# Two 64-row matmuls on different rows of the array for the low weights' half chunk of a score sum

## The chip, the core and the metric

The kernel runs on one core of one Trainium2 chip. The core has five engines with queues of their own: TensorE (PE, with its weight loads shown as PEld), VectorE (DVE), ScalarE (ACT), GpSimd (POOL, which here issues the gathers) and SyncE (SP, which issues the plain loads and stores). All DMA queues share 16 DMA engines. The metric is the device time of one execution in microseconds (us).

## What is computed

The input is x, 2048 tokens of 576 numbers. The output mixes two branches with a gate per token:

```python
g = sigmoid((x * gate_w).sum(-1, keepdims=True))
a = irfft2(rfft2(x) * (w_r + 1j * w_i))             # over tokens and features
q = einsum("nd,dhc->nhc", x, w_q)                   # 32 heads, 2 x 128 each
s1 = einsum("nhd,ed->nhe", q[..., :128], k1)        # 64 scores
s2 = einsum("nhd,ed->nhe", q[..., 128:], k2)        # 64 scores
e  = argmax(s1) * 64 + argmax(s2)                   # one expert per token and head
act = gelu(einsum("nd,nhd->nh", x, u[e]))
b = einsum("nh,nhd->nd", act, v[e])
out = g * a + (1 - g) * b
```

(The softmax runs over a single candidate, so its weight is 1.) An argmax that falls on another expert would change the output, so the scores need nearly full fp32 accuracy. u and v are stored side by side, so one gathered row of 1152 numbers serves both.

## The kernel before

**Tiles and chunks.** The tokens make 16 tiles t of 128. The 32 heads make 8 chunks c of 4 heads, so a chunk has 4 x 2 x 64 = 512 scores for a token. The 576 features make four chunks i = 0 to 3 of 128 and a half chunk i = 4 of 64.

**Weights.** `build_m(c, i)` multiplies the query weights by the keys into M, feature rows by 512 score columns, so that scores = x M. It works in fp32 on column halves of the array (the output on partitions 0 to 63 or 64 to 127, line p<-kT,uv in the profile). M is kept in two fp32r parts, `mh` (the rounded value) and `ml` (the rest); tiles named mhx and mlx are the same thing in other buffers. For i = 4 the 64 feature rows are laid down twice (`load_wq` copies them), so partitions 0 to 63 and 64 to 127 of `mh` hold the same, and of `ml` too.

**Tokens.** `load_x(b, i)` loads the transposed x for a block b of 512 tokens and splits it in the same way: ACT writes the rounded part (line 417), DVE the rest (line 418). For i < 4 these are two tiles. For i = 4 they share one tile, xts[8]: rounded part on partitions 0 to 63, rest on 64 to 127.

**Scores.** `scores(c, tp)` does two tiles, the members j = 0 and 1 of pair tp, into one PSUM buffer of two banks, a bank for each member. There are 8 x 8 = 64 such pairs. For i < 4 a member has three matmuls of 128 tokens by 512 columns (x hi with mh, x hi with ml, x lo with mh). For i = 4 it has two: the stacked tile with `mh` gives hi and lo at once, and the stacked tile with `ml` gives hi with ml (and the negligible lo with ml). That makes 14 matmuls for a member and 28 for a pair, 1792 in all. The token tile is the stationary operand, so each matmul loads 128 columns of weights first. Behind the matmuls stand a maximum on DVE (line 503), sign marks on ACT (line 511) and the search for the index of the maximum.

**Experts.** `group(t, c)` gathers four rows (line 637, tiles 0 to 9), `quad(t, c)` does it for tiles 10 to 15 (line 744; none is issued before the last score pair has begun). DVE takes the dot product with x (lines 649 and 753). The sum over v goes through DVE (line 681), or through a scaling on ACT and an addition on DVE (lines 674 and 675, the groups in `A_OF`), or through TensorE with a diagonal matrix: full width (128*128) for most groups in `D_OF`, on 64 columns for the tiles in `PAIR` (0 and 1), on 32 columns for the quads.

**The Fourier branch** (`fold`, `unit_front`, `unit_back`, `invert`) runs behind the scores, beside the quads.

**The order.** All steps are jobs made by `plan(...)`, with an assumed duration. A long list, `ORDER`, then says in which order they are issued; each engine takes its own jobs strictly in that order. The assumed durations were used to find the list and change no instruction. The 64 score pairs, the weight products and the diagonal matmuls thus stand in one fixed row on TensorE.

Of the kernel before, what the change touches and what calls it, by code (L numbers as in the profile page):

```python
# [19 lines left out]
P = 128  # L20
# [82 lines left out]
FIRST = 1.0  # L103
# [155 lines left out]
def act(n):  # L259
    return 0.1 + n / 1250  # L260
# [10 lines left out]
def load(nbytes, row):  # L271
    return nbytes / row * (0.01 + row * 0.0000363) / 16
# [3 lines left out]
def tile_kernel(ctx, tc, xn, xT, x5, wqT, wq5, kT, wri, uv, gw, t_kr, t_ff, t_fv, t_tw, t_io, out):  # L276
# [131 lines left out]
    def load_x(b, i, at, at2, n=1):  # L408
        st = buf("uv", ROW, view=lambda x: x.rearrange("p a d -> p (a d)")[:, : n * 512])
        h = P if i < 4 else E  # L410
        src = lambda: xT[:, i, b * 512 : (b + n) * 512] if i < 4 else x5[:, b * 512 : (b + n) * 512]
        ld(load(h * n * 2048, n * 2048) * FIRST, at, lambda: nc.sync.dma_start(st.ap[:h], src()), [st])
        for m in range(n):
            hi = xts[i if i < 4 else 8][b + m]
            lo, r = (xts[4 + i][b + m], 0) if i < 4 else (hi, E)
            cut = lambda m=m: st.ap[:h, m * 512 : m * 512 + 512]
            ac(act(512), at2, lambda hi=hi, cut=cut: actv(hi.ap[:h], cut(), AF.Copy), [hi], [st])  # L417
            dv(dve(512), at2, lambda hi=hi, lo=lo, cut=cut: vt(lo.ap[r : r + h], cut(), hi.ap[:h].bitcast(F32), ALU.subtract), [lo], [st, hi])
# [54 lines left out]
    def scores(c, tp, at):  # L473
# [6 lines left out]

        def part(j, i):
            t = 2 * tp + j
            b = t // 4
            tsl = slice((t % 4) * P, (t % 4) * P + P)
            mh, ml = m_t[c, i]
            x = xts[i if i < 4 else 8][b]
            seq = [(x, mh), (x, ml)] + ([(xts[4 + i][b], mh)] if i < 4 else [])

            def go():
                for n, (xx, m) in enumerate(seq):  # L490
                    mm(ps.ap[:, j, :], xx.ap[:, tsl], m.ap, start=i == n == 0, stop=i == 4 and n == len(seq) - 1)

            use = {id(q): q for pair in seq for q in pair}
            return plan("PE", 0.2275 * len(seq), at, go, [(ps, j)], list(use.values()))

        seq = [(j, i) for i in range(ND) for j in range(2)] if tp in (0, 7) else [(j, i) for j in range(2) for i in range(ND)]
        js = [part(j, i) for j, i in seq]
# [45 lines left out]
        for a, b, kind in runs(ta, tb):  # L543
# [3 lines left out]
            elif kind == "pair":  # L547
                for j, q, to, at_ in halves_of(ei[c], a, b):
                    ac(0.15, at + O_EI, lambda a=a, b=b, j=j, q=q, to=to: actv(
                        to(), fe.ap[64 * j : 64 * j + 64, a - ta : b - ta, q::2], AF.Copy, scale=float(E)), [(ei[c], t, j, q) for t in range(a, b)], [fe])  # L550
# [38 lines left out]
    def soften(c, t0, t1, at):  # L589
# [5 lines left out]
        def move():  # L595
            for a, b, kind in runs(t0, t1):
# [3 lines left out]
                else:  # L600
                    for j, q, to, _ in halves_of(moved, a, b):
                        ac(0.15, at, lambda a=a, b=b, j=j, q=q, to=to: actv(
# [27 lines left out]
    def group(t, c, at, ahead, gate_by=(), ks=range(HPC), mixed=False):  # L630
# [58 lines left out]
        for h in range(2 if t in PAIR else 0):  # L689
            dg = buf("dg", [P, 2, P // 2])  # L690
            for j in range(2):
                ac(0.2, at + O_DG, lambda j=j, h=h, dg=dg: actv(dg.ap[:, j, :], ip, AF.Copy, scale=a.ap[:, 2 * j + h : 2 * j + h + 1]), [(dg, j)], [a, "ip"])
# [459 lines left out]
A_OF = {2: (0, 1, 4), 3: (6,), 4: (3,), 5: (0, 2, 4, 7), 6: (0, 1, 2, 3, 4), 9: (0,)}  # L1152
# [276 lines left out]
```

## Time and profile before

| | |
|---|---|
| median of 3 runs | 937.85 us (936.73 to 946.15) |
| the profiled execution | 938.13 us |
| its span, first to last instruction | 936.4 us |
| busy, share of the span: PE / DVE / ACT / POOL | 91% / 88% / 70% / 60% |
| moved by DMA | 345.77 MB, of it 302.02 MB by gathers |
| HBM traffic over the span | 368 GB/s |

Busy time of PE is to be read with care: matmuls are pipelined, the record of a 128x512 matmul is about 0.39 us long while the next one starts after 0.23 us. So the prediction goes by distances between starts. In a timeline row stand the start, the length and the number of merged instructions; a form such as 128*64 128x288 means 128 rows and 64 columns of the array, and 288 columns streamed. An fp32 matmul leaves two records, an fp32r matmul one. PEld rows are the weight loads.

### The profile page before, as it was taken

The page shows a single profiled execution, that of the slowest core. Times are in us where ns is not written, and L with a number is a line of the kernel's source. Part 1 is how long each engine was busy: PE and PEld are TensorE (multiplying, and loading weights), DVE is VectorE, ACT ScalarE, POOL GpSimd, SP SyncE. Part 2 cuts the span into 40 slices and gives each one's busy share as a digit, 9 for nine tenths or more (in the row PEclk, how much of TensorE's full clock was granted, in tenths as well). Part 3 has the DMA queues.
Part 4 walks back from the last instruction along what each step waited for, and adds up shares of the span by engine and source line. Part 5 has one row for each costly group of instructions (what it writes and reads, how often), then busy time and mean ns, then how long its engine had stood idle before and what let it go on. Part 6 is the DMA issues. An engine that isn't in the chain of part 4 may idle for free.

```text
span 936.4 us, 17794 instructions
## 1 busy us (share of the span) xinstructions
PE 853.8 (91%) x5878; PEld 634.9 (68%) x5878; DVE 821.0 (88%) x1997; ACT 653.4 (70%) x2292; POOL 559.9 (60%) x516
## 2 busy tenths in 40 slices
PE   6999999999999999999999984687788779899997
PEld 5687887887877887887877872454455446566775
DVE  3585899999899999999989998998788889998887
ACT  3799999788887797977787899736338272634633
POOL 0234465665567666656656764777676667557762
PEclk9999999999999999999999997889899989999999
DMA  8967989989999999999999999999999999999998
GB/s 277 366 226 232 373 315 339 376 324 378 361 308 412 403 354 396 365 379 330 380 331 406 345 385 398 365 406 398 409 369 417 420 416 417 417 403 387 413 419 356
DMA packets 91261, 345.77 MB, mean 369 GB/s; under 512 B 10208, under 2 KB 10848, under 8 KB 91168
## 3 DMA queue, kind: packets, MB, share of 16 engines
q0 software_dynamic: 73728, 302.02, 83.7%
q1 hardware_dynamic: 17440, 42.60, 12.8%
q8 instruction: 47, 0.77, 0.3%
q14 instruction: 46, 0.38, 0.1%
HBM read 339.86 MB, written 4.72 MB: 368 GB/s over the span
## 4 chain that ended last, share of the span: by engine, by line
PE 60%; DMA 14%; DVE 12%; ACT 7%; issue 4%; POOL 2%; SPq 0%; DVEq 0%; ACTq 0%; POOLq 0%
PE p L346 60%; DMA uv<-uv,eiq 9%; DVE uv L753 4%; DMA uv<-xT 2%; ACT xr L734 2%; POOL uv L744 2%; ACT sg L511 2%; DMA uv<-uv,ei 1%; DVE uv L649 1%; DVE xn L681 1%; DMA xn<-xn 1%; DVE t L968 1%; DVE t L969 1%; POOL uv L637 1%; DMA uv<-wqT 1%
## 5 line engine op out<-in xcount | busy, mean ns | idle before, releaser
L637 POOL DMA_INDIRECT uv<-uv,ei x320 | 353.0, 1103 | 267.7 <-PE p L346 55.9
L346 PE MATMUL p<-mh,xt 128*128 128x512 f32 x768 | 263.4, 398 | 0.0
L744 POOL DMA_INDIRECT uv<-uv,eiq x192 | 206.7, 1077 | 93.4 <-PE p L346 39.3
L511 ACT ACTIVATE sg<-p,mx 128x64 bf16<-128x64 f32 x1024 | 230.9, 349 | 27.7 <-DVE mx L503 25.1
L649 DVE SCALAR_TENSOR_TENSOR uv<-uv,xn 128x576 f32<-128x576 f32 x320 | 232.8, 751 | 17.4 <-DMA uv<-uv,ei 13.9
L346 PE MATMUL p<-uv,dg 128*32 128x288 f32 (+2 forms) x1264 | 167.5, 430 | 41.6 <-DVE dg L759 23.3
L346 PE MATMUL p<-ml,xt 128*128 128x512 f32 x448 | 175.1, 391 | 1.0 <-DVE ml L467 1.0
L346 PEld LDWEIGHTS p<-mh,xt 128*128 128x128 f32 x768 | 144.2, 188 | 33.7 <-issue 3.1
L753 DVE SCALAR_TENSOR_TENSOR uv<-uv,xr 128x576 f32<-128x576 f32 x192 | 139.7, 754 | 18.8 <-DMA uv<-uv,eiq 18.2
L346 PEld LDWEIGHTS p<-uv,dg 128*32 128x32 f32 (+2 forms) x1264 | 85.6, 135 | 103.2 <-DVE dg L759 33.0
L346 PE MATMUL p<-mhx,xt 128*128 128x512 f32 x384 | 135.6, 400 | 0.9 <-ACT xt L417 0.9
L681 DVE SCALAR_TENSOR_TENSOR xn<-uv,a,xn 128x576 f32<-128x576 f32 x132 | 107.2, 812 | 2.3 <-ACT xn L677 1.3
L346 PEld LDWEIGHTS p<-ml,xt 128*128 128x128 f32 x448 | 84.2, 188 | 17.5 <-DVE ml L467 1.4
L503 DVE TENSOR_REDUCE mx<-p 128x16 f32<-128x1024 f32 x64 | 78.0, 1219 | 10.8 <-PE p L346 10.6
L346 PEld LDWEIGHTS p<-mhx,xt 128*128 128x128 f32 x384 | 72.0, 188 | 21.7 <-issue 3.5
L522 ACT ACTIVATE sg<-sg 128x256 bf16<-128x256 bf16 x192 | 75.3, 425 | 1.1
L346 PE MATMUL p<-mlx,xt 128*128 128x512 f32 x192 | 75.1, 391 | 0.0
L756 ACT ACTIVATE b<-z 128x4 f32<-128x4 f32 x48 | 9.9, 205 | 82.8 <-DVE uv L753 82.6
L734 ACT ACTIVATE xr<-xl 32x576 f32<-32x576 f32 x96 | 65.4, 681 | 1.4
L346 PEld LDWEIGHTS p<-kT,uv 128*64 128x64 f32 x1280 | 42.2, 143 | 19.5 <-issue 7.8
L346 PE MATMUL p<-kT,uv 128*64 128x64 f32 x1280 | 47.2, 230 | 6.9 <-ACT kT L787 6.3
L346 PE MATMUL p<-kr,f 128*32 128x128 f32 (+1 forms) x384 | 44.3, 328 | 9.5 <-DVE f L899 8.3
(127 smaller groups left out, 1139.8 us busy)
## 6 DMA issues: line engine op xcount, KB each, us to landing
uv<-wqT SPq DMA_DIRECT2D x32, 512.0 KB, 7.2
uv<-uv,ei POOLq DMA_INDIRECT x320, 6.8
w<-wri SPq DMA_DIRECT2D x16, 289.0 KB, 6.2
out<-xn SPq DMA_DIRECT2D x16, 288.0 KB, 5.6
uv<-uv,eiq POOLq DMA_INDIRECT x192, 7.8
xn<-xn SPq DMA_DIRECT2D x8, 288.0 KB, 5.3
tw<-t_tw SPq DMA_DIRECT2D x9, 256.0 KB, 6.7
uv<-xT SPq DMA_DIRECT2D x8, 256.0 KB, 6.9
```

The lines of the kernel that those rows point to most:

```text
L346: after("PE", nc.tensor.matmul(*args, **kw))
L503: dv(dve(1024, True), at + O_MAX + nd("m", c, tp), lambda: nc.vector.tensor_reduce(mv.ap[:, 2 * tp : 2 * tp + 2, :], ps.ap.rearrange("p a ...
L511: on("ACT", actv(sg.ap[:, j, g, :], ps.ap[:, j, g * E : g * E + E], AF.Sign, bias=mv.ap[:, 2 * tp + j, g : g + 1], scale=-1.0))
L522: ac(act(256), at + O_ADD, lambda b=b: actv(s2()[:, :, b * Q : b * Q + Q], s2()[:, :, b * Q : b * Q + Q], AF.Copy, bias=b / 4), [sg], [])
L637: on("POOL", nc.gpsimd.indirect_dma_start(out=g.ap.rearrange("p a d -> p (a d)"), out_offset=None, in_=uv, in_offset=bass.IndirectOffsetOn ...
L649: dv(0.68, at + O_DOT + nd("d", t, c), lambda k=k, g=rows[k], xk=xk: stt(g.ap[:, 0, :], g.ap[:, 0, :], 1.0, xk.ap, op0=ALU.mult, op1=ALU.m ...
L681: dv(0.73, at + O_SUM + nd("v", t, c), lambda v=v, s=s: stt(y.ap, v(), s(), y.ap, op0=ALU.mult, op1=ALU.add), [y], [(rows[k], 1), a])
L734: ac(0.69, at + 0.6 * j, lambda j=j, q=q: actv(xr[t][j].ap[QB * q : QB * q + QB, :], x.ap[QB * j : QB * j + QB, :], AF.Copy), [(xr[t][j], ...
L744: on("POOL", nc.gpsimd.indirect_dma_start(out=g.ap.rearrange("p a d -> p (a d)"), out_offset=None, in_=uv, in_offset=bass.IndirectOffsetOn ...
L753: dv(0.68, at + O_QDOT + nd("d", t, c), lambda j=j: stt(rows[j].ap[:, 0, :], rows[j].ap[:, 0, :], 1.0, xr[t][j].ap, op0=ALU.mult, op1=ALU. ...
L756: ac(0.12, at + O_QGELU, lambda: actv(b.ap, z.ap, AF.Gelu_apprx_tanh), [b], [(z, j) for j in range(HPC)], table="gelu")
L968: dv(dve(578, True), at, lambda: vt(a.ap, p.ap[:, :, :DF], w.ap[:, 0:1, :].to_broadcast([P, 2, DF]), ALU.mult), [(a, 0), (a, 1)], [p, w])
```

## The change

Three things change in the program. The half chunk's tile xts[8] is laid out by member: for the even tile of a pair the rounded part is on partitions 0 to 63 and the rest on 64 to 127, for the odd tile it is the other way round. The input x5 is stored accordingly (128 partitions of 256 columns a block, where it was 64 of 512), and two ACT and two DVE instructions of half the width make the split where one of each did. In `scores` the two steps for i = 4 become one, `both()`, at the end of the pair: a full matmul with `mh` for each member, then for each member a matmul with `ml` over 64 rows alone, rows 0 to 63 for j = 0 and rows 64 to 127 for j = 1, into their two banks. Third, `ORDER` is another list, and two groups, (2, 4) and (6, 1), leave `A_OF`. Some assumed durations (FIRST, 0.15 to 0.2, 0.2 to 0.24) change, which changes no instruction by itself.

```diff
     def load_x(b, i, at, at2, n=1):
-        h = P if i < 4 else E
-        src = lambda: xT[:, i, b * 512 : (b + n) * 512] if i < 4 else x5[:, b * 512 : (b + n) * 512]
...
+        w = 512 if i < 4 else 256
+        src = lambda: (xT[:, i] if i < 4 else x5)[:, b * w : (b + n) * w]
...
+            if i == 4:
+                x = xts[8][b + m]
+                of = lambda j, r, x=x: x.ap[E * r : E * r + E].rearrange("p (a j q) -> p a j q", j=2, q=P)[:, :, j, :]
+                own = lambda j, cut=cut: cut()[E * j : E * j + E].rearrange("p (a q) -> p a q", q=P)
+                for j in range(2):
+                    ac(act(256), at2, lambda j=j, of=of, own=own: actv(of(j, j), own(j), AF.Copy), [x], [st])
+                for j in range(2):
+                    dv(dve(256), at2, lambda j=j, of=of, own=own: vt(of(j, 1 - j), own(j), of(j, j).bitcast(F32), ALU.subtract), [x], [st])
+                continue
...
     def scores(c, tp, at):
...
-            seq = [(x, mh), (x, ml)] + ([(xts[4 + i][b], mh)] if i < 4 else [])
+            seq = [(xb(i), mh), (xb(i), ml), (xb(4 + i), mh)]
...
+        def both():
+            mh, ml = m_t[c, 4]
+            x = xb(8)
+            def go():
+                for j in range(2):
+                    mm(ps.ap[:, j, :], x.ap[:, tsl[j]], mh.ap, start=False, stop=False)
+                for j in range(2):
+                    mm(ps.ap[:, j, :], x.ap[E * j : E * j + E, tsl[j]], ml.ap[E * j : E * j + E], start=False, stop=True)
+            return plan("PE", 0.2275 * 3, at, go, [(ps, 0), (ps, 1)], [x, mh, ml])
...
-        seq = [(j, i) for i in range(ND) for j in range(2)] if tp in (0, 7) else [(j, i) for j in range(2) for i in range(ND)]
-        js = [part(j, i) for j, i in seq]
+        seq = [(j, i) for i in range(4) for j in range(2)] if tp in (0, 7) else [(j, i) for j in range(2) for i in range(4)]
+        js = [part(j, i) for j, i in seq] + [both()]
...
-A_OF = {2: (0, 1, 4), 3: (6,), 4: (3,), 5: (0, 2, 4, 7), 6: (0, 1, 2, 3, 4), 9: (0,)}
+A_OF = {2: (0, 1), 3: (6,), 4: (3,), 5: (0, 2, 4, 7), 6: (0, 2, 3, 4), 9: (0,)}
```

More of the change, by code (lines that the diff above doesn't have):

```diff
@@ L102 @@
 WINDOW, LOW, HIGH = 3.4133, 0.52, 0.86
-FIRST = 1.0
+FIRST = 1.1
 LAND = {'POOL': 0.2, 'SP': 5.29}
@@ L408, in load_x @@
     def load_x(b, i, at, at2, n=1):
-        st = buf("uv", ROW, view=lambda x: x.rearrange("p a d -> p (a d)")[:, : n * 512])
-        h = P if i < 4 else E
-        src = lambda: xT[:, i, b * 512 : (b + n) * 512] if i < 4 else x5[:, b * 512 : (b + n) * 512]
-        ld(load(h * n * 2048, n * 2048) * FIRST, at, lambda: nc.sync.dma_start(st.ap[:h], src()), [st])
-        for m in range(n):
[L414 to L418, printed above, removed]
+        w = 512 if i < 4 else 256
+        h = P
+        st = buf("uv", ROW, view=lambda x: x.rearrange("p a d -> p (a d)")[:, : n * w])
+        src = lambda: (xT[:, i] if i < 4 else x5)[:, b * w : (b + n) * w]
+        ld(load(P * n * w * 4, n * w * 4) * FIRST, at, lambda: nc.sync.dma_start(st.ap, src()), [st])
+        for m in range(n):
+            cut = lambda m=m: st.ap[:, m * w : m * w + w]
+            if i == 4:
[7 more added lines that the diff above has]
+                continue
+            hi, lo, r = xts[i][b + m], xts[4 + i][b + m], 0
+            ac(act(512), at2, lambda hi=hi, cut=cut: actv(hi.ap, cut(), AF.Copy), [hi], [st])
+            dv(dve(512), at2, lambda hi=hi, lo=lo, cut=cut: vt(lo.ap, cut(), hi.ap.bitcast(F32), ALU.subtract), [lo], [st, hi])
     def load_xn(t, tag, at, after=()):
@@ L479, in scores @@
         ps = psum()
+        tsl = [slice((2 * tp + j) % 4 * P, (2 * tp + j) % 4 * P + P) for j in range(2)]
+        xb = lambda i: xts[i][tp // 2]
         def part(j, i):
@@ L483, in part @@
             b = t // 4
-            tsl = slice((t % 4) * P, (t % 4) * P + P)
             mh, ml = m_t[c, i]
-            x = xts[i if i < 4 else 8][b]
-            seq = [(x, mh), (x, ml)] + ([(xts[4 + i][b], mh)] if i < 4 else [])
+            seq = [(xb(i), mh), (xb(i), ml), (xb(4 + i), mh)]
             def go():
                 for n, (xx, m) in enumerate(seq):
-                    mm(ps.ap[:, j, :], xx.ap[:, tsl], m.ap, start=i == n == 0, stop=i == 4 and n == len(seq) - 1)
+                    mm(ps.ap[:, j, :], xx.ap[:, tsl[j]], m.ap, start=i == n == 0, stop=False)
             use = {id(q): q for pair in seq for q in pair}
             return plan("PE", 0.2275 * len(seq), at, go, [(ps, j)], list(use.values()))
-        seq = [(j, i) for i in range(ND) for j in range(2)] if tp in (0, 7) else [(j, i) for j in range(2) for i in range(ND)]
-        js = [part(j, i) for j, i in seq]
+        def both():
[9 more added lines that the diff above has]
+        js = [part(j, i) for j, i in seq] + [both()]
         score_jobs[c, tp] = js
@@ L548, in scores @@
                 for j, q, to, at_ in halves_of(ei[c], a, b):
-                    ac(0.15, at + O_EI, lambda a=a, b=b, j=j, q=q, to=to: actv(
+                    ac(0.2, at + O_EI, lambda a=a, b=b, j=j, q=q, to=to: actv(
                         to(), fe.ap[64 * j : 64 * j + 64, a - ta : b - ta, q::2], AF.Copy, scale=float(E)), [(ei[c], t, j, q) for t in range(a, b)], [fe])
@@ L601, in move @@
                     for j, q, to, _ in halves_of(moved, a, b):
-                        ac(0.15, at, lambda a=a, b=b, j=j, q=q, to=to: actv(
+                        ac(0.2, at, lambda a=a, b=b, j=j, q=q, to=to: actv(
                             to(), cand.ap[64 * j : 64 * j + 64, a - t0 : b - t0, q::2], AF.Copy, bias=1.0), [(moved, a, j, q)], [cand])
@@ L691, in group @@
             for j in range(2):
-                ac(0.2, at + O_DG, lambda j=j, h=h, dg=dg: actv(dg.ap[:, j, :], ip, AF.Copy, scale=a.ap[:, 2 * j + h : 2 * j + h + 1]), [(dg, j)], [a, "ip"])
+                ac(0.24, at + O_DG, lambda j=j, h=h, dg=dg: actv(dg.ap[:, j, :], ip, AF.Copy, scale=a.ap[:, 2 * j + h : 2 * j + h + 1]), [(dg, j)], [a, "ip"])
             def go(h=h, dg=dg):
@@ L1403, in _layout @@
     arrays = {
-        "xn": xn, "xT": c(xt[: 4 * P].reshape(4, P, S).transpose(1, 0, 2)), "x5": c(xt[4 * P :]),
+        "xn": xn, "xT": c(xt[: 4 * P].reshape(4, P, S).transpose(1, 0, 2)), "x5": c(xt[4 * P :].reshape(E, 8, 2, P).transpose(2, 0, 1, 3).reshape(P, 8 * P)),
         "wqT": c(w[..., : 4 * P].reshape(NCH, P, 8, 4, P).transpose(0, 3, 1, 2, 4)), "wq5": c(w[..., 4 * P :].reshape(NCH, P, 512)), "kT": c(np.concatenate([k1, k2, k1], 1)), "wri": c(wri),
```

352 rows, old and new, of the table ORDER are left out of this document.

## The prediction, made before the result was known

> **What bounds the kernel now.** I read the windows first (two stretches, cut at the last score matmul), then the timeline of PE around that cut, then the starts of single matmuls.
>
> ```profile
> core 0: us, PE busy (x) PEld busy (x) DVE busy (x) ACT busy (x) POOL busy (x), PEclk, DMA share, GB/s
> 45.00:558.00 513.00, 512.24 (x3242) 402.08 (x3243) 474.99 (x1076) 432.98 (x1719) 308.50 (x280) 1.00 0.94 351
> 558.00:936.00 378.00, 306.58 (x2337) 204.84 (x2335) 327.59 (x890) 194.36 (x504) 246.41 (x228) 0.95 1.01 401
> ```
>
> ```profile
> 44.86 200.78 PE p L346 x1379
> ...
> 269.27 265.86 PE p L346 x1636
> ```
>
> ```profile
> 557.68 0.39 PE L346 MATMUL p<-ml,xt 128*128 128x512 f32 x1
> ```
>
> ```profile
> 599.15 0.94 POOL L744 DMA_INDIRECT uv<-uv,eiq  x1 [1.40 <-PE p L346]
> ```
>
> From 45 to 558 us TensorE is without a hole (512.24 of 513 us, granted clock 1.00), and the chain of waits goes through it in two long pieces of 200.78 and 265.86 us. At 557.68 the last score matmul starts. The quads of the six late tiles follow, the first at 599.15. In that second stretch PE has holes (306.58 of 378), DMA has none (share 1.01) and moves 401 GB/s, against 351 before. So TensorE sets when the scores are done, and DMA the length of what comes behind. A microsecond that a score pair gains or loses on PE moves the cut, and the rest of the kernel follows as far as its work is locked to the scores.
>
> **The price of a matmul inside a dense row.** The four groups of score matmuls count 768 + 448 + 384 + 192 = 1792, that is 28 for each of 64 pairs.
>
> ```profile
> L346 PE MATMUL p<-mh,xt 128*128 128x512 f32 x768 | 263.4, 398 | 0.0
> L346 PE MATMUL p<-ml,xt 128*128 128x512 f32 x448 | 175.1, 391 | 1.0 <-DVE ml L467 1.0
> L346 PE MATMUL p<-mhx,xt 128*128 128x512 f32 x384 | 135.6, 400 | 0.9 <-ACT xt L417 0.9
> L346 PE MATMUL p<-mlx,xt 128*128 128x512 f32 x192 | 75.1, 391 | 0.0
> ```
>
> ```profile
> 307.43 0.39 PE L346 MATMUL p<-mhx,xt 128*128 128x512 f32 x1
> ...
> 308.79 0.39 PE L346 MATMUL p<-mhx,xt 128*128 128x512 f32 x1
> ```
>
> From 307.43 to 308.79 are six steps: 1.36 / 6 = 0.227 us each. The records are 0.39 us long, but 0.227 is what a matmul costs.
>
> **The change, step 1: one streaming time saved.** A pair now sends its two `ml` matmuls one behind the other, 0.454 us. If two 64-row halves run side by side they take 0.227. The saving is 0.227 a pair, 64 x 0.227 = 14.5 us.
>
> **Step 2: going to half rows and back.** No matmul of this trace uses fewer than 128 rows, so the price of the switch has to be bounded. The nearest rows are those that use half the columns: the diagonal matmuls of tiles 0 and 1. They stand between score matmuls, in blocks of 8 and of 16 records.
>
> ```profile
> 293.74 0.39 PE L346 MATMUL p<-mhx,xt 128*128 128x512 f32 x1
> 294.06 1.19 PE L346 MATMUL p<-uv,dg 128*64 128x288 f32 x8
> 295.18 0.50 PE L346 MATMUL p<-mhx,xt 128*128 128x512 f32 x1
> 295.52 0.40 PE L346 MATMUL p<-mlx,xt 128*128 128x512 f32 x1
> ```
>
> ```profile
> 355.60 0.39 PE L346 MATMUL p<-mh,xt 128*128 128x512 f32 x1
> 355.92 2.16 PE L346 MATMUL p<-uv,dg 128*64 128x288 f32 x16
> ...
> 358.35 0.40 PE L346 MATMUL p<-ml,xt 128*128 128x512 f32 x1
> ```
>
> ```profile
> 294.06 0.68 PEld L346 LDWEIGHTS p<-uv,dg 128*64 128x64 f32 x8 [0.35 <-issue]
> 295.18 0.19 PEld L346 LDWEIGHTS p<-mhx,xt 128*128 128x128 f32 x1 [0.44 <-issue]
> 295.29 0.19 PEld L346 LDWEIGHTS p<-mlx,xt 128*128 128x128 f32 x1
> ```
>
> From the score matmul ahead of the block to the second one behind it are 295.52 - 293.74 = 1.78 us; without the two score matmuls (0.454) the block of 8 costs 1.326. The block of 16 costs 358.35 - 355.60 - 0.454 = 2.296. The difference, 0.97, is the streaming of 8 records, so each block pays 1.326 - 0.97 = 0.356 us beside its streaming. The same matmuls at full width show that the switch is what costs:
>
> ```profile
> 302.24 0.40 PE L346 MATMUL p<-mhx,xt 128*128 128x512 f32 x1
> 302.48 1.13 PE L346 MATMUL p<-uv,dg 128*128 128x288 f32 x4
> 303.23 0.61 PE L346 MATMUL p<-mh,xt 128*128 128x512 f32 x1
> 303.68 0.39 PE L346 MATMUL p<-ml,xt 128*128 128x512 f32 x1
> ```
>
> ```profile
> 331.72 0.39 PE L346 MATMUL p<-ml,xt 128*128 128x512 f32 x1
> 331.95 2.10 PE L346 MATMUL p<-uv,dg 128*128 128x288 f32 x8
> ...
> 334.12 0.39 PE L346 MATMUL p<-mlx,xt 128*128 128x512 f32 x1
> ```
>
> Here 4 records cost 303.68 - 302.24 - 0.454 = 0.986 and 8 cost 334.12 - 331.72 - 0.454 = 1.946: 0.24 a record and 0.026 left over. Two things follow. Column halves do run side by side (8 records in 0.97 us instead of 1.92). And nothing is paid at full width, since weights are loaded under the matmul ahead. At a switch they aren't: the first weight load starts at 294.06, 0.32 us behind the start at 293.74, so 0.09 us after that stream has ended; on the way back the load starts at 295.18 and the next load at 295.29, so 128 columns of weights take an open 0.11 us.
>
> For half rows the lower end is no price at all (loads go on in the background, only the rows differ), the upper end the same switch with more load in the open: the stationary operand has 128 columns where the blocks had 64, so half of 0.11 comes on top: 0.356 + 0.055 = 0.41 us. If the second half's load waits for the first, another 0.11. I take 0.41, since the column halves are the only partial use of the array here. A pair's tail then takes 0.41 + 0.227 = 0.637 where it took 0.454: +0.183 us, 64 x 0.183 = +11.7 us. The saving is eaten above a switch price of 0.227.
>
> [...]
>
> **Step 3: switches that fall together.** Where a two-row step stands directly beside a column block, one way back and one way in become one, half of 0.356, some 0.18 us less.
>
> ```profile
> L346 PE MATMUL p<-kT,uv 128*64 128x64 f32 x1280 | 47.2, 230 | 6.9 <-ACT kT L787 6.3 <-DMA uv<-wqT 0.7
> L346 PE MATMUL p<-uv,dg 128*64 128x288 f32 x256 | 40.3, 434 | 9.7 <-ACT dg L692 9.7
> ```
>
> There are 1280 / 32 = 40 weight products and 256 / 8 = 32 diagonal blocks, 72. With 9 steps to a pair, 128 of 576 places border a two-row step; at random 16 would meet, fewer since some blocks stand together. I take 11: -2 us.
>
> **Step 4: the layout of the half chunk.** The bytes loaded and the number of issues on SP stay. ACT and DVE get one more instruction for each of four token blocks.
>
> ```profile
> L418 DVE TENSOR_TENSOR xt<-uv,xt 128x512 fp32r<-128x512 f32 (+1 forms) x20 | 13.2, 687 | 18.0 <-ACT xt L417 18.0
> ```
>
> One of 512 columns takes 0.687; two of 256 take between 0.687 and twice that, so 0 to 0.7 us a block. Only the first block can be on the path (PE's dense row begins at 45 us; the others are loaded under it): 0 to 0.7, I take +0.2.
>
> **Step 5: two groups leave A_OF.** Eight ACT scalings go, eight DVE additions become multiply-adds.
>
> ```profile
> L674 ACT ACTIVATE uv<-uv,a 128x576 f32<-128x576 f32 x56 | 40.9, 784 | 3.1 <-DVE a L662 2.9
> L675 DVE TENSOR_TENSOR xn<-uv,xn 128x576 f32<-128x576 f32 x56 | 42.1, 752 | 0.9 <-ACT uv L674 0.3
> L681 DVE SCALAR_TENSOR_TENSOR xn<-uv,a,xn 128x576 f32<-128x576 f32 x132 | 107.2, 812 | 2.3 <-ACT xn L677 1.3
> ```
>
> ACT loses 8 x 0.784 = 6.3 us, DVE gains 8 x (0.812 - 0.752) = 0.5 us of its 475 in 513. PE covers both: 0. Without that cover, +0.5.
>
> **Step 6: the new order.** It moves every queue's jobs, POOL's and SP's too, but makes no new work. In the first stretch PE has no hole that an order could close. In the second DMA is full. I give it 0, between -4 and +4: that is 1% of the 378 us behind the cut, whose DMA rows are at their limit; a worse order would show as holes there.
>
> **The sum.** The cut moves by 11.7 - 2 + 0.2 = +9.9. What is behind it keeps its length, because each engine's order is fixed: dots, diagonal matmuls and gathers take their turns between the score pairs. From the profiled execution (span 936.4, 1.7 around it, 938.1; 0.3 above the median 937.85): 938.1 + 9.9 = 948.0 us.
>
> **The rivals.**
>
> No drain for rows (faster). Half rows are loaded in the background and the whole 14.5 us come: the mechanism is that only the rows differ and no column's path does. For it: column halves run side by side at full gain once they run. Against: loads at a switch of columns wait. It decides below a price of 0.227. The cut moves by -14.5; DVE then has 475 in 498 (95%) and DMA must give 351 x 513 / 498 = 362 GB/s, under the 401 seen. Between all of it and two thirds: 924 to 929. [...]
>
> One side only. The way in is hidden, the way back costs its 0.09 + 0.11 = 0.20: 0.227 - 0.20 leaves 0.03 a pair, -2 us: 936. For it: nothing seen; against: both ways wait in the column rows.
>
> Dearer. The two loads go one behind the other: +0.11 x 64 = 7 us, 955. Or the halves don't run side by side, so that the saving fails: +14.5, 962.5.
>
> Absorbed. PE loses 10 us, but gathers go on meanwhile and fewer are left behind the cut.
>
> ```profile
> POOL uv L637 <- PE p L346: 55.6, 43, 5.1
> ```
>
> ```profile
> q0 software_dynamic: 73728, 302.02, 83.7%
> ...
> L637 POOL DMA_INDIRECT uv<-uv,ei x320 | 353.0, 1103 | 267.7 <-PE p L346 55.9
> ...
> L744 POOL DMA_INDIRECT uv<-uv,eiq x192 | 206.7, 1077 | 93.4 <-PE p L346 39.3
> ```
>
> In the first stretch 280 of the 320 gathers of line 637 are issued, so up to 40 come later; a gather is 302.02 / (320 + 192) = 0.59 MB, or 1.5 us of DMA at 401 GB/s. Seven more of them done would give back all 10 us: 938 to 941. Against: POOL waited 55.6 us there for buffers that PE frees, in PE's fixed order.
>
> **How the numbers follow.** Forecast 0.42 (own range 943 to 953); dearer 0.18 (953 to 963); absorbed 0.09; one side 0.11; no drain 0.20 (924 to 930). About 1% (9.4 us) is what a measurement can tell from no change; the border at 947.2 runs through the forecast, two thirds of it above. Slower by over 1%: 0.28 + 0.18 = 0.46. Within 1%: 0.14 + 0.09 + 0.11 = 0.34. Faster: 0.20. The range, 929 to 962, takes in the top of the fast case and nearly all of the dear one.
>
> **What would show it.** Step 1: the two 64-row matmuls start within some 10 ns. Step 2: the 64-row weight load starts 0.3 us behind the last full matmul, and from that matmul to the second one behind the pair it is 0.637 + 0.454 = 1.09 us; 0.68 would mean no drain. Step 3: fewer than 64 such ways back. The sum: the last score matmul at about 568 us, with no hole on PE before it, and some 378 us behind it. The prediction is wrong if PE's row gets holes, if the half rows load in the background, or if the part behind the cut changes its length by more than 4 us.

## The result and the profile after

The changed kernel took 946.78 us in the median of 12 runs (946.09 to 953.36). The kernel before, timed beside it, took 939.75 (12 runs, 936.73 to 946.15). The ratio is 1.0085 with a 95% interval of 1.0068 to 1.0103, so the change costs 7 us. The forecast was 948.0.

The profiled execution of the changed kernel took 949.5 us, 2.7 above its own median. The one of before (938.13) is 1.6 under its median. The two profiles are therefore further apart (11.4 us) than the kernels.

The windows of the changed kernel, cut at its last score matmul as those of before were (columns: length, then busy us and instructions of each engine, granted clock, DMA share, GB/s):

```profile
45.00:568.70 523.70, 520.62 (x3247) 388.70 (x3245) 477.50 (x1074) 427.83 (x1711) 303.53 (x282) 1.00 0.93 346
568.70:947.30 378.60, 309.47 (x2338) 208.23 (x2336) 325.20 (x892) 194.23 (x504) 246.78 (x228) 0.92 1.01 400
```

Its timeline of PE, first at the last score step, then around the two-row step of one pair, with the weight loads of the same place:

```profile
568.50 0.50 PE L346 MATMUL p<-ml,xt 64*128 64x512 f32 x2
```

```profile
103.02 0.84 PE L346 MATMUL p<-mh,xt 128*128 128x512 f32 x3
103.80 0.50 PE L346 MATMUL p<-ml,xt 64*128 64x512 f32 x2
104.23 0.50 PE L346 MATMUL p<-mh,xt 128*128 128x512 f32 x1
104.56 0.39 PE L346 MATMUL p<-ml,xt 128*128 128x512 f32 x1
```

```profile
103.79 0.18 PEld L346 LDWEIGHTS p<-ml,xt 64*128 64x128 f32 x2 [0.35 <-issue]
104.22 0.19 PEld L346 LDWEIGHTS p<-mh,xt 128*128 128x128 f32 x1 [0.25 <-issue]
104.33 0.19 PEld L346 LDWEIGHTS p<-ml,xt 128*128 128x128 f32 x1
```

The last score matmul starts at 568.50, 10.8 us later than before. PE is nearly as dense as it was up to there: its holes are 523.7 - 520.62 = 3.1 us, against 0.8 in the kernel before. What follows is as long as it was (378.6; before 378.5 from its cut at 557.9). So most of the loss lies in PE's own work, ahead of the cut.

The step itself reads so. The third matmul of the merged row ends at 103.02 + 0.84 = 103.86, so it starts 0.39 earlier, at 103.47. The 64-row load comes at 103.79, 0.32 us later, with nothing but [<-issue] as the reason for the idle time. The two half matmuls share one row of 0.50 us, as long as one of them alone, so they start together; in the records of all 64 pairs the second starts 3 or 4 ns behind the first. The load on the way back is at 104.22, the second full matmul at 104.56: 1.09 us from 103.47, where four matmuls in a dense row take 4 x 0.227 = 0.91.

### The profile page after: what moved, and what is told of

It reads as the page before. It is cut to its first block, busy times and chain, and to the rows that moved or that the text cites. A ratio compares the mean times of both kernels' runs of the same rounds, so it can differ in the third digit from the quotient of the medians.

```text
span 947.3 us, 17772 instructions
## 1 busy us (share of the span) xinstructions
PE 864.8 (91%) x5878; PEld 623.9 (66%) x5878; DVE 820.5 (87%) x2001; ACT 649.2 (69%) x2288; POOL 554.2 (59%) x516
## 4 chain that ended last, share of the span: by engine, by line
PE 54%; DMA 16%; DVE 12%; ACT 10%; issue 4%; POOL 2%; SPq 0%; DVEq 0%; ACTq 0%; POOLq 0%
PE p L346 54%; DMA uv<-uv,eiq 7%; DMA uv<-uv,ei 6%; DVE uv L775 3%; ACT xr L756 3%; DMA uv<-xT 2%; ACT sg L533 2%; DVE uv L671 2%; POOL uv L659 1%; POOL uv L766 1%; DVE xn L703 1%; ACT fl L952 1%; DMA uv<-wqT 1%; DVE xn L1122 1%; ACT uv L696 1%
## 5 line engine op out<-in xcount | busy, mean ns | idle before, releaser
L659 POOL DMA_INDIRECT uv<-uv,ei x320 | 346.6, 1083 | 285.3 <-PE p L346 74.8
L346 PE MATMUL p<-mh,xt 128*128 128x512 f32 x768 | 257.2, 401 | 1.2 <-ACT mh L467 0.6
L671 DVE SCALAR_TENSOR_TENSOR uv<-uv,xn 128x576 f32<-128x576 f32 x320 | 234.0, 752 | 21.5 <-DMA uv<-uv,ei 16.8
L346 PE MATMUL p<-ml,xt 128*128 128x512 f32 (+1 forms) x448 | 157.2, 422 | 0.1
L346 PE MATMUL p<-mhx,xt 128*128 128x512 f32 x384 | 138.2, 407 | 0.5 <-ACT xt L426 0.3
L703 DVE SCALAR_TENSOR_TENSOR xn<-uv,a,xn 128x576 f32<-128x576 f32 x140 | 113.8, 814 | 1.5 <-ACT xn L699 0.2
L346 PEld LDWEIGHTS p<-ml,xt 128*128 128x128 f32 (+1 forms) x448 | 72.1, 187 | 33.7 <-issue 21.6
L346 PE MATMUL p<-kr,f 128*32 128x128 f32 (+1 forms) x384 | 47.0, 337 | 2.3 <-DVE f L921 1.6
```

The lines of the kernel that those rows point to most:

```text
L346: after("PE", nc.tensor.matmul(*args, **kw))
L659: on("POOL", nc.gpsimd.indirect_dma_start(out=g.ap.rearrange("p a d -> p (a d)"), out_offset=None, in_=uv, in_offset=bass.IndirectOffsetOn ...
L671: dv(0.68, at + O_DOT + nd("d", t, c), lambda k=k, g=rows[k], xk=xk: stt(g.ap[:, 0, :], g.ap[:, 0, :], 1.0, xk.ap, op0=ALU.mult, op1=ALU.m ...
L703: dv(0.73, at + O_SUM + nd("v", t, c), lambda v=v, s=s: stt(y.ap, v(), s(), y.ap, op0=ALU.mult, op1=ALU.add), [y], [(rows[k], 1), a])
```

## The experiments

Four runs went to one chip, on which the kernel before took 939.69 us. All later runs went to another, on which it took 976 to 992 us; those are read against the kernel before of the same chip. "Cut" is the start of the last score matmul in the profile.

**Undo the half rows.** In the last step of the changed kernel:

```diff
-                    mm(ps.ap[:, j, :], x.ap[E * j : E * j + E, tsl[j]], ml.ap[E * j : E * j + E], start=False, stop=True)
+                    mm(ps.ap[:, j, :], x.ap[:, tsl[j]], ml.ap, start=False, stop=True)
```

> The changed kernel, order and layout included, with the two products of ml over all 128 rows again (the stacked tile with ml, as before), so 28 full matmuls a pair and no half rows. Theory A (the loss is the price of switching between full and half rows, 0.41 us a pair against 0.227 saved): each pair's tail takes 0.18 us less, 64 x 0.18 = 11.5, less about 1 us since five of the switches met a column block; 946.8 - 10.5 = 936 us, the last score matmul at about 558 us. Rival B (the half rows cost nothing; the loss came with the new order and layout): 946 to 948 us.

Measured: 939.21 us, ratio to the kernel before 0.9994 (0.9974 to 1.0014); cut at 561.3. The new order and layout with full matmuls are as fast as the old, so Rival B is out: the half rows carry the whole loss of 946.78 - 939.21 = 7.6 us. But 7.6 is less than the 10.5 expected. The cut came only 7.2 us earlier than in the changed kernel. Here PE waits, in us in total, times, longest, from 45 us to the cut:

```profile
PE p L346 <- ACT sg L533: 1.7, 3, 1.2
PE p L346 <- ACT mh L467: 0.9, 2, 0.8
PE p L346 <- ACT dg L725: 0.7, 1, 0.7
PE p L346 <- ACT mlx L474: 0.6, 1, 0.6
```

These rows of the waits view sum to 3.9 us. The changed kernel has 2.7 up to its own cut, and the kernel before 0.8:

```profile
PE p L346 <- ACT sg L533: 1.9, 3, 1.2
PE p L346 <- ACT mlx L474: 0.5, 1, 0.5
PE p L346 <- ACT dg L725: 0.3, 1, 0.3
```

So the waits are some 1.2 us of what is missing; the rest is not explained. The profiled execution of e1_full took 944.42 us, 5.2 above its median, so its cut is a late one.

**The saving without the price.**

```diff
-                for j in range(2):
-                    mm(ps.ap[:, j, :], x.ap[E * j : E * j + E, tsl[j]], ml.ap[E * j : E * j + E], start=False, stop=True)
+                mm(ps.ap[:, 0, :], x.ap[:, tsl[0]], ml.ap, start=False, stop=True)
```

> Like e1_full, but the product of the half chunk's rounded x with ml is left out for the odd member of each pair: 27 full matmuls, no half rows. It is what the change would cost if two half rows took one streaming time and the switch nothing. Theory A (what TensorE loses or gains in the score stage passes to the end): 64 x 0.227 = 14.5 us under e1_full, so 921.5 us if A is right on e1_full. Rival C (DVE or DMA take over as the bound once PE is faster): 926 us or more, with holes in PE's row before the last score matmul.

Measured: 933.63 us, ratio 0.9924 (0.9898 to 0.9951), 5.6 us under e1_full; cut at 552.9. Of 14.5 us taken from PE, 5.6 reach the end. In the two profiles the cut comes 8.4 us earlier and the executions are 8.6 apart (935.85 and 944.42), so the profiles are further apart than the medians; behind the cut both are as long (380.6 and 380.8). The longest waits of PE up to the cut:

```profile
PE p L346 <- ACT mh L467: 3.4, 2, 2.1
PE p L346 <- ACT sg L532: 2.6, 4, 1.2
PE p L346 <- ACT dg L724: 1.2, 1, 1.2
PE p L346 <- ACT dg L713: 1.1, 2, 0.5
```

ACT ends these (8.3 us here, 3.9 in e1_full), and in the window up to the cut ACT is busy 426.51 of 508.1 us and DMA's share is 0.95:

```profile
45.00:553.10 508.10, 499.25 (x3182) 394.05 (x3180) 475.07 (x1073) 426.51 (x1708) 307.52 (x280) 1.00 0.95 356
```

So Rival C was right about the size and the holes. The instructions that end PE's waits are ACT's, which it had not named, but that does not rule out DVE or DMA behind them. ACT itself waits in this window mostly for DVE, and so it did just ahead of PE's longest wait:

```profile
ACT b L674 <- DVE uv L670: 27.9, 21, 5.4
ACT sg L532 <- DVE mx L524: 21.2, 20, 3.3
```

```profile
456.39 0.93 ACT L532 ACTIVATE sg<-p,mx 128x64 bf16<-128x64 f32 x4 [2.59 <-DVE mx L524]
```

```profile
458.98 0.50 PE L346 MATMUL p<-mh,ident 128*128 128x256 f32 x2 [2.08 <-ACT mh L467]
```

Whether ACT's own fixed order or DVE ahead of it makes the holes was not tried.

**The same switch, one half only.** As e2_one_full, with `x.ap[:E, ...]` and `ml.ap[:E]` for the one matmul that is left.

> Like the changed kernel, but the ml product of the odd member is left out: one 64-row matmul a pair, on rows 0 to 63, so it has the same switches and no second half. It differs from e2_one_full only in the rows of that one matmul. Theory A (the halves run wholly side by side; the price is the switch): the same time as the changed kernel, 946 to 948 us, and 64 x 0.41 = 26 us, less about 1, above e2_one_full. Rival D (part of the price is the second half, its load or its streaming): shorter than the changed kernel by up to 14.5 us, 932 us at the least.

Measured: 947.05 us, ratio 1.0084 (1.0054 to 1.0115). That is the time of the changed kernel, so the second half costs nothing. It is 13.4 us over e2_one_full, where 25 to 26 were expected. On PE the price is what was expected:

```profile
102.23 0.61 PE L346 MATMUL p<-mh,xt 128*128 128x512 f32 x2
102.78 0.50 PE L346 MATMUL p<-ml,xt 64*128 64x512 f32 x1
103.21 0.50 PE L346 MATMUL p<-mh,xt 128*128 128x512 f32 x1
103.54 0.39 PE L346 MATMUL p<-ml,xt 128*128 128x512 f32 x1
```

The last full matmul starts at 102.23 + 0.61 - 0.39 = 102.45, the second one behind the half at 103.54: 1.09 us with one half as with two. Without a switch these three steps take 0.68, so the price is 0.41. In time it shows as about half. In part that is because e2_one_full could not use its saving: up to the cut PE has 8.9 us of holes there and 3.2 here. The rest of the difference was not followed.

**The change in the old order.** The kernel before with only the new layout and the half rows, sent behind the last step of the pair:

```diff
+                if i == 4:
+                    mm(ps.ap[:, j, :], x.ap[:, tsl], mh.ap, start=False, stop=False)
+                    seen.append(j)
+                    for k in range(2 if len(seen) == 2 else 0):
+                        u = (2 * tp + k) % 4 * P
+                        mm(ps.ap[:, k, :], x.ap[E * k : E * k + E, u : u + P], ml.ap[E * k : E * k + E], start=False, stop=True)
+                    return
```

> The kernel before, with its order, A_OF and assumed durations, and only the half chunk's layout and the two 64-row matmuls of the change: they are sent right behind whichever of the two members' last steps comes second. Theory A with the new order counted in: the score pairs pay 64 x 0.18 = 11.5 us, less 0.2 for each place where the two-row step meets a column block; the old order has 55 separate column blocks before the last score matmul where the new one has 42 (at 0.35 us each the new order saves 4.6 us): 939.75 + 11.5 - 1 = 950 us. Rival E (the orders are worth the same): 946 to 948 us. Rival B (half rows free): 940 us.

Measured: 948.97 us, ratio 1.0090 (1.0062 to 1.0118); cut at 568.1, 10.4 us later than in the kernel before. In the old order 9.3 us of the loss reach the end (the cuts are of single profiles, the times medians). That the new order is worth the 2.2 us between 948.97 and 946.78 is not shown: the two intervals overlap widely.

**Two switches a pair.**

```diff
                 for j in range(2):
                     mm(ps.ap[:, j, :], x.ap[:, tsl[j]], mh.ap, start=False, stop=False)
-                for j in range(2):
                     mm(ps.ap[:, j, :], x.ap[E * j : E * j + E, tsl[j]], ml.ap[E * j : E * j + E], start=False, stop=True)
```

> The changed kernel with the four matmuls of the last step in another sequence: full for the even member, its 64 rows, full for the odd member, its 64 rows. Two ways in and two ways back a pair, and no half runs beside the other. Theory A (every way in and back is paid, whatever stands around it): a pair takes another 0.41 + 0.227 = 0.637 us less about 0.003, 64 x 0.634 = 40.6 us on PE; the last score matmul at 568.5 + 40.6 = 609 us and the time 947 + 40 = 987 us. Rival F (a switch is paid once for a pair, by the first matmul of another form): only the lost overlap, 64 x 0.227 = 14.5 us, 961 us. Rival G (the stretch behind the scores gets shorter as gathers go on meanwhile): last score matmul at 609 us, but 975 us or less.

Measured: 1029.88 us where the kernel before took 986.15, ratio 1.0426 (1.0373 to 1.0480).

```profile
113.05 0.50 PE L346 MATMUL p<-ml,xt 64*128 64x512 f32 x1
113.47 0.49 PE L346 MATMUL p<-mh,xt 128*128 128x512 f32 x1
113.90 0.49 PE L346 MATMUL p<-ml,xt 64*128 64x512 f32 x1
114.32 0.50 PE L346 MATMUL p<-mh,xt 128*128 128x512 f32 x1
```

Every change between half and full rows costs again: 0.42 to 0.43 us from start to start where a dense row has 0.227. Rival F is out. Theory A put it 47 us above the kernel before (987 against 939.7); it is 43.7. Rival G is out too: the last score matmul starts at 618.7 and 416.5 us follow, where the kernel before, profiled on this chip, has 574.0 and 412.9.

**Both halves on the same rows.** `x.ap[:E, ...]` and `ml.ap[:E]` for both members.

> The changed kernel with both 64-row matmuls on rows 0 to 63. For the odd member these rows hold the rest of x, so its product is rest with ml and the product of the rounded part with ml is left out. Same number of switches, same banks. Theory A (the halves overlap because their rows differ): the second streams behind the first, 64 x 0.227 = 14.5 us more, 961 us, the two starting 0.2 us apart in the records instead of 0.003. Rival H (they overlap because they write different banks or simply because they are small): 947 us.

> The kernel of e6_same_rows once more, for the same reason. Theory A (the halves overlap because their rows differ): from the last full matmul of a pair to the second one behind the pair 1.31 us where the changed kernel has 1.09, 64 x 0.224 = 14.3 us more; 947 + 14 = 961 us if the kernel before takes 939.7, or 21.5 us over it. Rival H: 1.09 us and 7 us over it.

Measured: 1013.22 and 1005.35 us, ratios 1.0273 (1.0220 to 1.0325) and 1.0283 (1.0243 to 1.0322).

```profile
108.52 0.84 PE L346 MATMUL p<-mh,xt 128*128 128x512 f32 x3
109.29 0.73 PE L346 MATMUL p<-ml,xt 64*128 64x512 f32 x2
109.95 0.50 PE L346 MATMUL p<-mh,xt 128*128 128x512 f32 x1
110.28 0.40 PE L346 MATMUL p<-ml,xt 128*128 128x512 f32 x1
```

The pair of halves now lasts 0.73 instead of 0.50, and from 108.97 to 110.28 are 1.31 us, as expected. It is the different rows that let the halves run together, not the different banks, which this kernel has as well; Rival H is out. Whether one bank would do as well was not tried. The time went up by 27 to 29 us over the kernel before, more than the 21.5 expected. In the two profiles the cuts (595.8 and 596.5) are 22 us later than the 574.0 of the kernel before on this chip, and what follows is not longer (405.4 and 409.4 us against 412.9). So the profiles do not show the extra 6 to 7 us; what made them up was not followed.

**One full matmul more, and one less, in the old order.** For the odd member's half chunk:

```diff
-            seq = [(x, mh), (x, ml)] + ([(xts[4 + i][b], mh)] if i < 4 else [])
+            seq = [(x, mh), (x, ml)] + ([(xts[4 + i][b], mh)] if i < 4 else [(x, ml)] * j)
```

and for one less `(x, ml)` is left out where i = 4 and j = 1. The kernel before was profiled beside them.

> The kernel before with one more full matmul a pair: the odd member's stacked tile with ml is added a second time. 29 full matmuls, no half rows, everything else as before. It asks how much of 14.5 us that PE takes longer reaches the end. Theory A (a loss on PE passes whole, since PE's row has no holes): 939.7 + 14.5 = 954 us. Rival G (gathers catch up meanwhile and the stretch behind the scores gets shorter): 940 to 948 us. Leaving one matmul out gave only 5.6 of 14.5 us; if a loss passes no better than that gain, 945 us.

> The kernel of e7_one_more once more, since its first runs were on a chip on which the kernel before took 986 us and where DMA was slower. Theory A (a loss on PE passes whole): the last score matmul at 557.7 + 14.5 = 572 us, and 14.5 us over the kernel before of the same chip (954 if that is 939.7). Theory A2 (it passes by four fifths or so, as in e4_old_order, where 9.3 of 10.7 came through): 11 to 12 us over it. Rival G (gathers catch up): 8 us or less over it.

> The kernel before, unchanged, for a profile on the same chip as the two runs beside it. Ratio 1. On a chip with the DMA of the first profile: last score matmul near 557.7 us, 378.7 us behind it. On a slower one the difference to 937.85 should lie behind the scores, where DMA is full, more than ahead of them.

> 29 full matmuls a pair in the old order, beside before_again (28) and e9_one_less (27). Theory A (a loss on PE passes whole): last score matmul 14.5 us behind that of before_again, and 14.5 us more in time. Theory A2: 11 to 12 us. Rival G (the stretch behind the scores gets shorter as gathers go on meanwhile): the last score matmul 14.5 us later and the time 8 us or less.

> The kernel before without the half chunk's ml product of the odd member: 27 full matmuls a pair in the old order, so 14.5 us less for PE. Theory J (PE's row is just dense: what is added passes, what is taken away opens waits for ACT and DVE): 4 to 7 us less, with 4 us or more of new holes in PE's row, as e2_one_full had it against e1_full. Theory A without a limit: 14.5 us less.

| kernel | full matmuls a pair | cut | behind it | ratio to the kernel before |
|---|---|---|---|---|
| e9_one_less | 27 | 570.2 | 414.2 | 0.9958 (0.9922 to 0.9995) |
| before_again | 28 | 574.0 | 412.9 | 1.0030 (0.9984 to 1.0077) |
| e7_third | 29 | 581.4 | 409.7 | 1.0023 (0.9981 to 1.0065) |
| e7_one_more | 29 | 586.3 | 415.7 | 1.0115 (1.0063 to 1.0166) |
| e7_again | 29 | 577.6 | 402.5 | 1.0083 (1.0046 to 1.0121) |

These five do not answer the question for the first chip, because on the second one PE's row isn't dense. The kernel before there, up to its cut and behind it:

```profile
45.00:574.30 529.30, 518.62 (x3240) 402.97 (x3239) 474.29 (x1073) 432.18 (x1716) 304.18 (x280) 1.00 0.93 340
574.30:986.90 412.60, 319.88 (x2337) 211.96 (x2335) 327.08 (x892) 195.16 (x506) 246.54 (x228) 0.91 0.97 368
```

PE stands still for 529.3 - 518.6 = 10.7 us ahead of the cut, against 0.8 on the first chip, and DMA moves 368 GB/s behind it instead of 401. Beside before_again, from the same round, the 14.5 us of e7_third move the cut by 7.4 only, and those taken away in e9_one_less move it by 3.8; the cuts of e7_again and e7_one_more, from other rounds, are 3.5 and 12.2 later. The three ratios of the kernel with one more range from 1.0023 to 1.0115, so on that chip 2 to 11 us of 14.5 come through; a better figure was not reached. The larger losses of e5_between and e6_same_rows came through about whole on the same chip, so this is no rule. All of 14.5 lies outside the intervals of e7_again and e7_third, and Rival G's cut, 14.5 us later, is not seen either. For one matmul less Theory J fits: about 4 us less (0.5 to 7.7), and 17.7 us of holes on PE against 10.7. before_again's expectation held: of the 50.5 us between the two spans 34 lie behind the cut and 16 ahead of it.

## Why the prediction was right, point by point

**The view of the bound** held. The cut moved, and the stretch behind it kept its length: 378.8 us in the changed kernel and 380.5 in e4_old_order, 378.7 before. One sign did not: PE's row was to have no hole before the cut and has 3.1 us from 45 us on. They do not carry the loss, since from the first score matmul to the cut the holes are 4.0 us against 4.5 before. "Absorbed" did not happen on the first chip.

**Step 1** held: the halves run side by side. Two of them last as long as one, and e3_one_half has the time of the changed kernel.

**Step 2** held in mechanism and size. The price was taken from 64-column blocks as 0.356 + 0.055 = 0.41 us; it measures 1.09 - 0.68 = 0.41. The load came 0.32 us behind the last full matmul, as read from the column blocks, and both 64-row loads go together, 3 or 4 ns apart, so "dearer" fell away too. The whole of the loss hangs on this term, since without the half rows the time is that of before (e1_full).

On the way in the load stands 0.32 - 0.227 = 0.09 us after the stream ahead has ended, with 0.227 for that stream, as the load of the column block at 294.06 does in the kernel before; no row shows what fills that time. The two half matmuls run beside each other, their starts 3 or 4 ns apart, but their loads do not start under the full matmul: in all 64 pairs the first stands 0.32 us or more behind its start.

**Step 3** was mis-sized. Five two-row steps stand directly ahead of a column block, not 11: -1 us, not -2. One of them shows what this is worth at best:

```profile
122.49 0.73 PE L346 MATMUL p<-mh,xt 128*128 128x512 f32 x2
123.15 0.49 PE L346 MATMUL p<-ml,xt 64*128 64x512 f32 x2
123.58 0.51 PE L346 MATMUL p<-kT,uv 128*64 128x64 f32 x10
```

The full matmul starts at 122.49 + 0.73 - 0.39 = 122.83 and the column block 0.75 later; directly behind a full matmul it would start 0.32 later, as the column block at 294.06 did behind 293.74 in the kernel before. So here the step adds 0.43 us, where two full `ml` matmuls would add 0.454. Even beside a column block half rows win only 0.02 us.

**Step 4** could not be seen in the layout but in the order. The new order loads the half chunk of x first, three loads ahead of everything else, and the first weight product starts at 9.30 us instead of 6.26. In e4_old_order, with the layout alone, it starts at 5.55. So the layout alone shows no later start. Whether +0.2 was right can't be told, as the kernel before itself starts at 6.26 and 5.71 in its two profiles. The loads on SP in the changed kernel, then that of the half chunk in the kernel before:

```profile
0.74 1.34 SPq L413 DMA_DIRECT2D uv<-x  x3
2.12 0.43 SPq L808 DMA_DIRECT2D kT<-kT  x1
```

```profile
5.70 0.60 SPq L412 DMA_DIRECT2D uv<-x  x1
```

**Step 5** was not tried by itself. e1_full has it too and ends where the kernel before does, so no loss of it shows.

**Step 6** was argued wrongly, without harm to the sum. "In the first stretch PE has no hole that an order could close" overlooked that an order also sets how often PE changes its form. Counted in the sequence of PE's instructions up to the cut, the column blocks form 55 separate runs in the old order and 42 in the new: an estimated 13 x 0.356 = 4.6 us less. The later start (+3.5, first score matmul at 14.7 instead of 11.2) would take most of it back. That e1_full ends where the kernel before does fits this, but its profile does not show it: with -4.6 and its own later start of +2.7 its cut should come 1.9 us earlier than in the kernel before, and it comes 3.6 later.

**The sum.** The cut: 64 x 0.18 = +11.5, step 3 -1.0, column runs -4.6, later start +3.5, makes +9.4; 1.4 of the measured 10.8 us is left unassigned. The forecast had +9.9, from fewer terms that partly made up for each other. The 4.6 is an estimate that no run measures. In time the change cost 7.0 and not 9.9, within the range. Where the other 2.9 us went is not shown: in the two profiles, 11.4 us apart, the move of the cut comes through whole.

That 948.0 lies so near 946.78 is in part luck. It stands on 938.1 for the kernel before; from the later median, 939.75, the same +9.9 would give 949.65. The prediction also gave its largest chance, 0.46, to a loss of over 1%; the measured 0.85% falls where it gave 0.34.

**The rivals.** "No drain" is out, since 1.09 us were measured and not 0.68, and its price was too good as well. e2_one_full is that case in effect, and it gains 5.6 us on e1_full and ends at 933.6, not at 924 to 929. The prediction let two thirds or more of a saving on PE pass, from DVE's busy share and DMA's rate; 5.6 of 14.5, about four tenths, passed, and the waits that open are ended by ACT, whose busy share had not been looked at. "One side only" is out by the load times on both sides: 103.79, 0.32 us behind the full matmul ahead, and 104.22, 0.42 us behind the halves at 103.80.

## What to carry to other kernels

In this kernel a step on part of the array cost a switch in and out of its form, 0.36 us for 64 columns and 0.41 us for 64 rows, beside its streaming. Such a step had to save more than that here, and it paid to keep steps of one form side by side: with the two halves of a pair apart it took 43.7 us more than the kernel before (second chip), with them together 7.0 (first chip). Leaving the work out and timing that shows the whole gain on offer before anything is built, here 6 us. Where PE was just dense, on the first chip, what was added came through nearly whole (9.3 of 10.4 us), while of what was taken away less than half did (5.6 of 14.5). Each stands on one kernel, and on the second chip only 2 to 11 of 14.5 added us came through.

## What the runs showed of the chip that was not expected

The price of the switch was nearly the same for rows as for columns, 0.41 and 0.36 us. The prediction put the 0.05 between them down to the longer weights, which no run varied. Two chips differ: the same kernel before took 939.7 us on one and, in three rounds, 976 to 992 on the other, with 401 and 368 GB/s behind the scores, and 0.8 and 10.7 us of holes in PE's row ahead of them. Which engine is dense, and so what a change is worth, is then another answer.
